# Where the TensorE fillers stand in a delta-rule recurrence: between its stages instead of behind them

## The chip, the cores and the metric

The kernel runs as one program on one core of a Trainium2 chip. The metric is the time of one execution on the device in microseconds (us); lower is better. Each engine (PE for TensorE, DVE for VectorE, ACT for ScalarE, POOL for GpSimd, SP for SyncE) takes its own instructions in the order in which they were written, and waits for other engines through semaphores.

## The reference

Three layers follow each other. The first is a recurrence over 768 tokens with a 48 x 48 state for each of 4 x 8 heads, the second a gated layer that mixes tokens, the third a gated two-layer network on neighbouring tokens.

```python
for t in range(S):                       # S = 768, B = 4, H = 8, D = 48
    y[:, :, t] = einsum('bhd,bhde->bhe', q[:, :, t], state)
    v_old = einsum('bhde,bhd->bhe', state, kt)          # kt: normalised key
    state = state + bt * einsum('bhd,bhe->bhde', kt, vt - v_old)
x = y as (B, S, 384)
h = gelu(x @ w_in)                       # 384 -> 1024, tanh form
u, v = halves of h
v_n = layer_norm(v) * g_ln
x = x + (u * (w_sg @ v_n + b_sg)) @ w_out
xk, xr = mixes of x and x one token earlier (mu_k, mu_r)
out = sigmoid(xr @ w_r) * (relu(xk @ w_k) ** 2 @ w_v)
```

## The kernel before

The recurrence is done in chunks of 64 tokens, 12 in all (`s` is 0 to 11), for two halves `o` of the 32 heads. Two chunks make a group `g` of 128 tokens, six groups in all. For a group TensorE first makes the products of its keys with each other, the Gram products (`gram`, lines 328 and 330: 64 small products for each of four quarters, each quarter in two halves `j`, copied out by ACT at line 337). VectorE then inverts a triangular matrix for each head (`solver`, background work in small pieces), and TensorE joins the result with the off-diagonal Gram blocks in two halves (`couple`, line 448, the halves of N).

For each chunk and half of the heads five stages run: `st_rq` (keys times state and keys times queries, lines 489 and 492), `st_d` (line 512), `st_n` (line 525), `st_s` (the state's update, line 540) and `st_y` (the output, line 554). Each is a burst of small products on TensorE, one 32 to 64 columns wide at a time, followed by one or two copies on ACT or DVE (`residual`, line 466, makes the operand of `st_d` from the result of `st_rq`). A float32 product of these counts twice in the trace.

The order on every engine is written by hand. Time is counted in points, 24 for a group. `run` emits one slot of three points: the stages of that slot, three calls of `tick` (which hands out background work: solver pieces, layer norm, weight rounding, and Gram products at fixed points), and at the end `fill(n)`, which emits n units of large products: `x @ w_in` of finished groups (lines 624 and 676), or, where none is ready, `keep_warm` products without use (line 715). A slot is planned for 5.315 us of TensorE time; what the stages leave of that is filled, and what is over or missing is carried on in `used[0]`. The slots of a group begin at points 0, 3, 6 ... 21, and take in turn `st_n` with `st_rq`, and `st_d` with `st_s` and `st_y`.

The weights `w_in`, `w_out` and `w_k` come in as 64-bit blocks and are rounded on the way by jobs (`narrow`): load to a tile `raw` by SP, four steps on DVE, one on POOL, a split on ACT and POOL, and for `w_out` and `w_k` a store back to DRAM by SP (`scratch`, line 197). After the recurrence come the token mixing (line 935), the projections (line 146) and the last network; the change moves nothing there.

## Time and profile before

| what | value |
|---|---|
| time, median of 3 runs | 782.36 us (777.26 to 782.89) |
| profiled execution | 785.0 us, of which the profile's span is 783.3 us |
| mean granted TensorE clock of the profiled execution | 0.961 of full speed |
| PE busy | 717.5 us of the span |
| recurrence, from the first slots to the last stage | about 54 to 349 us |

The span runs from the first to the last instruction. An execution takes some 2 us more than its span. Busy time of PE is a union of product times, of which neighbours overlap, so that a full 20 us in a window does not say that the products could not have been issued closer.

### The profile page before, as it was taken

The numbers are of one execution on the slowest core, as the hardware profiler recorded it, in microseconds if no ns is written. First come the engines' busy times: TensorE is split into PE (matmuls) and PEld (weight loads), VectorE is DVE, ScalarE is ACT, GpSimd is POOL, SyncE is SP. The second block draws the span as 40 slices with busy tenths as digits, with TensorE's granted clock in tenths as the row PEclk, the third lists the DMA queues.
The fourth block names the chain that finished last, engine by engine and source line by source line (L and its number), as shares of the span: only waits on it lengthen the run. The fifth ranks groups of instructions, "written<-read, shape, count | busy, mean of one in ns | idle before, by whom it ended". The sixth has DMA issues, their size and how long they took to land.

```text
span 783.3 us, 25096 instructions
## 1 busy us (share of the span) xinstructions
PE 717.5 (92%) x10898; PEld 658.0 (84%) x10898; DVE 504.7 (64%) x1071; ACT 373.2 (48%) x752; POOL 199.9 (26%) x246
## 2 busy tenths in 40 slices
PE   3479989899998999798889979999999999999998
PEld 3335768788887887686879969999999999999997
DVE  6997779779597895622265967269664564564441
ACT  2234566566766767753333332128463463452330
POOL 3143335344363564520216351201000000000000
PEclk9979999899799999999989989999999999999999
DMA  8312346365566647538367554228000000000000
GB/s 240 79 62 67 112 94 190 104 187 168 130 175 175 189 142 199 180 106 223 122 228 237 180 163 146 75 87 222 21 11 31 11 21 31 11 21 31 11 22 31
DMA packets 82159, 88.76 MB, mean 113 GB/s; under 512 B 24704, under 2 KB 65024, under 8 KB 82048
## 3 DMA queue, kind: packets, MB, share of 16 engines
q1 hardware_dynamic: 76816, 77.92, 33.8%
q0 software_dynamic: 4800, 9.04, 4.2%
q8 instruction: 85, 1.39, 0.8%
q10 hardware_dynamic: 432, 0.20, 0.1%
q14 instruction: 26, 0.21, 0.1%
HBM read 56.60 MB, written 25.82 MB: 105 GB/s over the span
## 4 chain that ended last, share of the span: by engine, by line
PE 75%; DMA 7%; DVE 7%; issue 3%; POOL 3%; ACT 2%; SPq 2%; POOLq 0%; DVEq 0%
PE ms L146 35%; PE ms L676 7%; PE ms L935 6%; PE ms L624 6%; PE ms L715 4%; PE ms L554 3%; PE rk L512 3%; PE rk L489 2%; PE rk L525 2%; PE sps L540 2%; PE ms L448 2%; PE ms L328 2%; DVE sg L350 1%; DMA raw<-in_w_r_dram 1%; POOL na L172 1%
## 5 line engine op out<-in xcount | busy, mean ns | idle before, releaser
L146 PE MATMUL ms<-wvh,sl 128*128 128x384 f32 x192 | 64.6, 336 | 0.0
L146 PE MATMUL ms<-wvl,sh 128*128 128x384 f32 x192 | 64.5, 336 | 0.0
L146 PE MATMUL ms<-wvh,sh 128*128 128x384 f32 x192 | 64.5, 336 | 0.0
L146 PE MATMUL ms<-xm_hi,sw0h 128*128 128x384 f32 x192 | 64.2, 335 | 0.0
L146 PE MATMUL ms<-xm_hi,sw0l 128*128 128x384 f32 x192 | 64.2, 334 | 0.0
L146 PE MATMUL ms<-xm_lo,sw0h 128*128 128x384 f32 x192 | 64.2, 334 | 0.0
L172 POOL TENSOR_TENSOR na<-na,raw 128x256 int32<-128x256 int32 (+2 forms) x43 | 38.3, 890 | 86.1 <-DVE na L170 80.4
L118 DVE TENSOR_TENSOR sl<-sg,sh 128x384 fp32r<-128x384 f32 x64 | 35.6, 557 | 30.3 <-ACT sh L115 30.2
L935 PE MATMUL ms<-sw0h,g 128*128 128x384 f32 x192 | 50.4, 336 | 2.1 <-DVE g L118 2.1
L115 ACT ACTIVATE sh<-sg 128x384 fp32r<-128x384 f32 x64 | 33.5, 524 | 36.3 <-DVE sg L1109 36.3
L935 PE MATMUL ms<-ws1h,g 128*128 128x384 f32 x192 | 49.9, 334 | 0.0
L676 PE MATMUL ms<-xh,wiu_hi 128*128 128x256 f32 x144 | 41.0, 303 | 6.9 <-ACT v L633 6.9
L1125 DVE TENSOR_TENSOR sg<-sg,ms 128x384 f32<-128x384 f32 x24 | 13.3, 554 | 46.2 <-PE ms L146 46.2
L1109 DVE TENSOR_TENSOR sg<-sg 128x384 f32<-128x384 f32 x64 | 35.3, 552 | 11.5 <-ACT sg L1108 11.4
L350 DVE TENSOR_TENSOR sg<-sg,Yt 128x512 f32<-128x512 f32 (+10 forms) x78 | 41.5, 532 | 1.6
L1108 ACT ACTIVATE sg<-ms 128x384 f32<-128x384 f32 x64 | 30.8, 481 | 24.2 <-PE ms L146 23.9
L676 PE MATMUL ms<-xl,wiu_hi 128*128 128x256 f32 x144 | 40.0, 297 | 2.4 <-issue 2.4
L115 ACT ACTIVATE gh<-w 128x384 fp32r<-128x384 f32 x32 | 16.6, 524 | 53.5 <-DVE w L1022 53.5
L676 PE MATMUL ms<-xh,wiu_lo 128*128 128x256 f32 x144 | 40.4, 299 | 0.1
L146 PE MATMUL ms<-gh,wo_hi 128*128 128x384 f32 x96 | 35.2, 366 | 5.7 <-ACT gh L115 5.7
L505 POOL TENSOR_SCALAR_AFFINE_SELECT SQ<-SQ 64x512 f32<-64x512 f32 x36 | 26.9, 746 | 48.0 <-ACT SQ L504 41.1
L676 PEld LDWEIGHTS ms<-xh,wiu_hi 128*128 128x128 f32 x144 | 27.7, 201 | 13.1 <-ACT v L633 8.2
(236 smaller groups left out, 2244.9 us busy)
## 6 DMA issues: line engine op xcount, KB each, us to landing
u_d<-ug SPq DMA_DIRECT2D x24, 256.0 KB, 4.1
u<-u_d SPq DMA_DIRECT2D x16, 384.0 KB, 5.5
vn_d<-v SPq DMA_DIRECT2D x22, 256.0 KB, 3.8
vk<-in_vk_dram SPq DMA_DIRECT2D x24, 192.0 KB, 3.9
vk<-in_vk_dram SPq DMA_DIRECT2D x12, 384.0 KB, 4.9
out_dram<-sg SPq DMA_DIRECT2D x24, 192.0 KB, 1.9
SQ<-in_q_d_dram SPq DMA_DIRECT2D x36, 96.0 KB, 3.6
xT<-yst SPq DMA_DIRECT2D x23, 144.0 KB, 3.8
```

What stands on the lines that cost most here:

```text
L115: A.activation(hi, src, AF.Copy)
L118: eng_lo.tensor_tensor(lo, src, hi.bitcast(F32), op=ALU.subtract)
L146: T.matmul(pt, lhsT=a, rhs=b, start=(i == 0), stop=(i == n - 1))
L172: G.tensor_tensor(a.bitcast(I32), a.bitcast(I32), w_lo.bitcast(I32), op=ALU.add)
L350: V.tensor_tensor(tv, vw(a_t, a_off, a_dims), vw(b_t, b_off, b_dims), op=ALU.mult)
L505: G.affine_select(out=pt, in_=pt, pattern=[[0, 8], [1, C]], compare_op=ALU.is_gt, fill=0.0, base=0, channel_multiplier=-1)
L624: T.matmul(vstat[g, b], lhsT=a[:, c], rhs=w[:, c], start=first, stop=last)
L676: T.matmul(vstat["u"][:, 2 * P * d:2 * P * d + 2 * P], lhsT=w[:, c, ds_], rhs=a[:, c].rearrange("p b t -> p (b t)"), start=first, stop=last)
L715: T.matmul(o, lhsT=warm, rhs=vw(warm, 0, [(0, 4), (1, P)]), start=True, stop=True)
L935: T.matmul(pt[:, :DM], lhsT=v[:, ds_], rhs=w, start=(c == 0 and i == 0), stop=(c == 5 and i == 2))
L1108: A.activation(r, pt[:, :DM], AF.Relu)
L1109: V.tensor_tensor(r, r, r, op=ALU.mult)
```

## The change

Nothing that is computed changes. Six edits go together:

- `run` emits the stages of a slot one after the other with a part of the filler behind each, where it emitted them together and all filler at the end. The filler of a slot is planned before it from the same costs, up to 15 units instead of 14, and split in equal parts (`gap`).
- The Gram halves and the halves of N are put in a list `batches` and emitted behind the three ticks of a slot, each followed by a part of the filler. A quarter's two halves, which followed each other, now have filler between them.
- Gram quarters come at points 13, 18, 21 and 23 of a group instead of 17, 19, 21 and 23. The plan counts them in every group, also in the last two, which have none.
- The two halves of N come 2 and 8 points after the end of the solver instead of 2 and 3.
- `raw` tiles of the rounding jobs get five buffers instead of three, in a pool of their own (`jp`), and the store of a rounded block is issued 4 points after its split instead of 2, without holding the job's place in the list of running jobs.
- The tiles `r32` and `u1` have one buffer instead of two.

```diff
-GRAM0 = 17
+GRAMS = (13, 18, 21, 23)
-PUT = 2
+PUT = 4
-GSTEP = 2
-LAGC = 2
+LAGC = (2, 8)
-NRAW = 3
+NRAW = 5
...
-            yield PUT, put
+            yield PUT, put, True
...
             for k in range(2):
-                after(LAGC + k, lambda k=k: couple(g, k))
+                after(LAGC[k], lambda k=k: join(g, k))
+
+        def join(g, k):
+            batches.append(lambda: couple(g, k))
...
-            t = ap2.tile([P, 8, D], F32, name="r32")
+            t = ap1.tile([P, 8, D], F32, name="r32")
...
-            u1 = RQs[o, "u"] = ap2.tile([P, 8, D], F32, name="u1")
+            u1 = RQs[o, "u"] = ap1.tile([P, 8, D], F32, name="u1")
...
-                        e[0] = point[0] + c[0]
+                        e[0] = point[0] + c[0] * (len(c) < 3)
...
-            if grams and (point[0] - GRAM0) % GSTEP == 0:
-                for _, f in grams.pop(0):
-                    f()
-                used[0] += 1.1
+            if grams and point[0] % 24 in GRAMS:
+                batches.extend(f for _, f in grams.pop(0))
             point[0] += 1
 
         def run(*todo):
-            bodies = [f(s, o) for f, s, o in todo]
-            used[0] += sum(COST[f.__name__[3:]] for f, _, _ in todo)
-            for _ in range(3):
-                for b in bodies:
-                    next(b, None)
+            n = point[0] % 24
+            plan = sum(k in GRAMS for k in range(n, n + 3)), n in (0, 6)
+            need = sum(COST[f.__name__[3:]] for f, _, _ in todo) + 1.1 * plan[0] + 1.4 * plan[1]
+            gap = min(max((SLOT - need + spare[0]) / 0.235, 3), 15)
+            spare[0] = min(spare[0] + SLOT - need - 0.235 * gap, 1)
+            gap /= len(todo) + 2 * plan[0] + plan[1] + (n < 3 and not todo)
+            bodies = []
+            for f, s, o in todo:
+                b = f(s, o)
+                next(b, None)
+                next(b, None)
+                bodies.append(b)
+                fill(gap)
+            for b in bodies:
+                next(b, None)
             for _ in range(3):
                 tick()
                 if early_items and point[0] >= FROM:
                     early_items.pop(0)()
-            n = min(max((SLOT - used[0]) / 0.235, 3), 14)
-            used[0] += n * 0.235 - SLOT
-            fill(n)
+            while batches:
+                batches.pop(0)()
+                fill(gap)
```

The order of instructions shows it at three places. The first is PE at the beginning of group 3 (point 0 and on), from the end of `st_rq` to the next stages; `ms<-DT,sg` is the product of N, `ms<-xh,wiu` and `ms<-wiv` are filler, `rk<-r,DT` is `st_d`, `sps` is `st_s`. Before:

```order
L489 MATMUL rk<-sw0h_120,kT_97 64x48
L492 MATMUL qk<-sw0h_120,kT_97 64x64
L489 MATMUL rk<-sw0l_121,kT_97 64x48
L492 MATMUL qk<-sw0l_121,kT_97 64x64
L448 MATMUL ms<-DT,sg_111 32x32 x64
L676 MATMUL ms<-xh,wiu_hi 128x256
L676 MATMUL ms<-xh,wiu_lo 128x256
L676 MATMUL ms<-xl,wiu_hi 128x256
```

Both halves of N, 64 products, stood in one piece; three more fillers and `st_d` followed. The same place on PE in the changed kernel:

```order
L629 MATMUL ms<-wiv_hi,xh 128x512
L629 MATMUL ms<-wiv_lo,xh 128x512
L454 MATMUL ms<-DT,sg_114 32x32 x32
L629 MATMUL ms<-wiv_hi,xl 128x512
L681 MATMUL ms<-xh,wiu_hi 128x256
L681 MATMUL ms<-xh,wiu_lo 128x256
L681 MATMUL ms<-xl,wiu_hi 128x256
L517 MATMUL rk<-r_3816,DT 32x48 x32
L681 MATMUL ms<-xh,wiu_hi 128x256
```

One half of N stands there, with two fillers ahead of it and four behind; the other half moved two slots on, and filler now also follows `st_d`.

The second place is PE at the end of `st_y` and the Gram quarter after it, in group 2 at points 21 to 23 (`ms<-sw0l` at lines 328 and 330, in the changed kernel 331 and 333, are Gram products, the lines at 676 and 629 filler). Before, its last three rows and the filler behind them:

```order
L330 MATMUL ms<-sw0l_96 32x64
L328 MATMUL ms<-sw0l_96 32x64
L330 MATMUL ms<-sw0l_96 32x64
L676 MATMUL ms<-xh,wiu_hi 128x256
L676 MATMUL ms<-xh,wiu_lo 128x256
L676 MATMUL ms<-xl,wiu_hi 128x256
```

All 64 Gram products of this slot end there in one piece; three more fillers and `st_n` followed. The same place on PE in the changed kernel, at its seam between the two quarters:

```order
L331 MATMUL ms<-sw0l_99 32x64
L333 MATMUL ms<-sw0l_99 32x64
L629 MATMUL ms<-wiv_hi,xl 128x512
L331 MATMUL ms<-sw0l_99 32x64
L333 MATMUL ms<-sw0l_99 32x64
```

A single filler stands between two pieces of 32 products each, and after the second piece `st_n` follows without filler.

The third place is SP in group 2, where it loads `raw` blocks and stores rounded ones (`wo_d<-raw`). Before:

```order
L197 DMA wo_d<-raw 256x1x192 x2
L682 DMA u_d<-ug 512x1x128 x2
L155 DMA raw<-in_w_out_dram 128x384
L155 DMA raw<-in_w_k_dram 128x512
L268 DMA vk<-in_vk_dram 64x768
```

The same stretch of SP's queue in the changed kernel:

```order
L201 DMA wo_d<-raw 256x1x192
L670 DMA vn_d<-v 128x512
L159 DMA raw<-in_w_k_dram 128x512
L670 DMA vn_d<-v 128x512
L201 DMA wo_d<-raw 256x1x192
```

Stores now stand one at a time between other transfers, and a load of a new block stands ahead of the store of an older one.

## Rows read from the trace of the kernel before

**Rows 1.** The page: busy time, the instruction queue of PE, the chain's shares.

```profile
PE 717.5 (92%) x10898; PEld 658.0 (84%) x10898; DVE 504.7 (64%) x1071; ACT 373.2 (48%) x752; POOL 199.9 (26%) x246
...
q8 instruction: 85, 1.39, 0.8%
...
PE 75%; DMA 7%; DVE 7%; issue 3%; POOL 3%; ACT 2%; SPq 2%; POOLq 0%; DVEq 0%
```

**Rows 2.** Windows, groups 1 to 5: length, engines' busy time, granted clock, DMA.

```profile
96.74:148.47 51.73, 46.77 (x1378) 39.22 (x1377) 43.34 (x99) 33.21 (x66) 22.30 (x27) 0.93 0.51 136
148.47:198.81 50.34, 45.92 (x1389) 40.03 (x1388) 39.59 (x95) 33.89 (x67) 21.92 (x29) 0.97 0.58 162
198.81:249.80 50.99, 47.86 (x1390) 42.69 (x1389) 41.35 (x94) 33.78 (x67) 22.18 (x28) 0.90 0.59 165
249.80:296.30 46.50, 46.47 (x1163) 40.75 (x1162) 39.28 (x92) 31.58 (x60) 25.85 (x29) 0.93 0.58 162
296.30:345.95 49.65, 44.98 (x1116) 37.32 (x1115) 23.40 (x44) 34.91 (x68) 22.73 (x33) 0.93 0.58 166
```

**Rows 3.** Waits of PE from 60 to 300 us: sum, times, longest.

```profile
PE ms L448 <- issue: 3.4, 2, 2.3
PE ms L328 <- issue: 3.2, 2, 2.0
PE ms L676 <- issue: 2.4, 1, 2.4
PE ms L330 <- issue: 1.4, 3, 0.7
PE ms L448 <- ACT sw0l L504: 1.3, 1, 1.3
...
PE ms L624 <- issue: 0.6, 1, 0.6
```

**Rows 4.** Timeline of PE: one such stop, inside a Gram quarter.

```profile
135.76 0.22 PE L330 MATMUL ms<-kT 64*32 64x64 f32 x1
137.97 0.24 PE L328 MATMUL ms<-kT 64*32 64x64 f32 x1 [1.98 <-issue]
```

**Rows 5.** Windows as in rows 2: a dense stretch, a clean one, one at half clock.

```profile
240.65:249.80 9.15, 6.02 (x264) 5.35 (x263) 8.46 (x11) 5.25 (x12) 2.57 (x2) 1.00 0.50 162
213.11:224.21 11.10, 11.10 (x260) 9.58 (x259) 8.86 (x18) 7.74 (x15) 6.63 (x7) 1.00 0.66 181
199.77:210.01 10.24, 10.24 (x304) 9.63 (x302) 7.72 (x34) 6.57 (x13) 3.64 (x8) 0.50 0.39 108
```

**Rows 6.** Timeline of PE: 14 fillers between two small stages, then another stage.

```profile
112.79 0.23 PE L492 MATMUL qk<-SQ,kT 64*64 64x64 f32 x2
112.95 0.50 PE L624 MATMUL ms<-wiv_hi,xh 128*128 128x512 f32 x1
113.28 0.40 PE L624 MATMUL ms<-wiv_lo,xh 128*128 128x512 f32 x1
...
116.03 0.39 PE L624 MATMUL ms<-wiv_lo,xh 128*128 128x512 f32 x1
116.34 0.88 PE L512 MATMUL rk<-r,DT 32*32 32x48 f32 x64
117.16 0.24 PE L540 MATMUL sps<-sw0h,vk 64*48 64x48 f32 x1
```

**Rows 7.** Timeline of PE: the stage of line 512 at half clock; nine keep-warm products.

```profile
105.26 1.50 PE L512 MATMUL rk<-r,DT 32*32 32x48 f32 x64
...
109.01 2.12 PE L715 MATMUL ms<-warm 128*128 128x512 bf16 x9
```

**Rows 8.** Timelines of PE and DVE: products of `st_rq` and the residual made of them.

```profile
225.94 0.23 PE L492 MATMUL qk<-SQ,kT 64*64 64x64 f32 x2
...
227.18 0.55 DVE L466 TENSOR_TENSOR r<-vk,rk 128x384 f32<-128x384 f32 x1
```

**Rows 9.** Timeline of PE behind the recurrence: the two long stops there.

```profile
371.96 0.39 PE L676 MATMUL ms<-xh,wiu_hi 128*128 128x256 f32 x1 [3.22 <-ACT v L633]
...
376.61 0.39 PE L676 MATMUL ms<-xh,wiu_hi 128*128 128x256 f32 x1 [2.25 <-ACT v L633]
```

**Rows 10.** Waits of SP from 54 to 300 us: stores of rounded blocks.

```profile
SPq L197 <- POOL raw L118: 31.1, 10, 6.5
```

More of the change, by code (lines that the diff above doesn't have):

```diff
@@ L105, in fused_kernel @@
     stg = ctx.enter_context(tc.tile_pool(name="stg", bufs=2))
+    fl = ctx.enter_context(ExitStack())
+    jp = fl.enter_context(tc.tile_pool(name="jp", bufs=2))
     xT = cp.tile([P, B, 3, S + 1], F32, name="xT")
@@ L147, in mm3, with narrow @@
                 i += 1
-    def narrow(dram, i, j, hi, lo, cw=CW, pool=stg, lag=JLAG, parts=None):
-        w = CW if pool is stg else cw
-        raw = pool.tile([P, 2 * w], U32, name="raw", bufs=NRAW if pool is stg else 2)
+    rounding = [jp]
+    def narrow(dram, i, j, hi, lo, cw=CW, lag=JLAG, parts=None):
+        pool = rounding[0]
+        w = CW if pool is jp else DM
+        raw = pool.tile([P, 2 * w], U32, name="raw", bufs=NRAW if pool is jp else 2)
         nc.sync.dma_start(out=raw[:, :2 * cw], in_=dram[i * P:(i + 1) * P, j:j + cw].bitcast(U32))
@@ L159, in narrow @@
         yield 0, lambda: A.activation(w_lo.bitcast(I32), w_lo, AF.Copy, scale=2.0 ** -29)
-        a = pool.tile([P, w], U32, name="na", bufs=NNA if pool is stg else 2)[:, :cw]
+        a = pool.tile([P, w], U32, name="na", bufs=NNA if pool is jp else 2)[:, :cw]
         af = a.bitcast(F32)
@@ L186, in resident, with scratch @@
                         for i in range(nblk) for j in range(j0, j1, CW)]
-    def scratch(dram, name, nblk, n, cw=CW, pool=stg):
+    def scratch(dram, name, nblk, n, cw=CW):
         d = dp.tile([nblk, P, 2, n], F32, name=name + "_d")
@@ L193, in job @@
             parts = []
-            yield from narrow(dram, i, j, None, None, cw, pool, parts=parts)
+            yield from narrow(dram, i, j, None, None, cw, parts=parts)
             def put():
                 nc.sync.dma_start(out=d[i, :, :, j:j + cw], in_=parts[0])
-            yield PUT, put
+            yield PUT, put, True
         return d[:, :, 0], d[:, :, 1], [lambda i=i, j=j: job(i, j) for i in range(nblk) for j in range(0, n, cw)]
@@ L218, in fused_kernel @@
     fp = tc.tile_pool(name="fp", bufs=2)
-    fl = ctx.enter_context(ExitStack())
     fp = fl.enter_context(fp)
@@ L451, in couple @@
                 A.activation(GL[r:r + 32, u0:u0 + NPR], w[r:r + 32], AF.Copy)
-            used[0] += 1.4
             joined.add(2 * g + k)
@@ L580, in store_x @@
                                     in_=yst[64 * h + e:64 * h + e + n, 6:8, :])
-        units, grams, opened, owed, splits, used = [], [], [[], None], [0], [], [0]
+        units, grams, opened, owed, splits, spare = [], [], [[], None], [0], [], [0]
         spent = [0, 0, 0]
@@ L755, in background @@
             debt[0] = min(t, 0) * (point[1] > 0)
-        running, debt = [], [0]
+        running, debt, batches = [], [0], []
         jobs = in_jobs + jobs
@@ L824, in tick @@
             point[1] = min(g, 1) + 1
-            gg, nn = divmod(point[0] - GRAM0, 24)
+            gg, nn = divmod(point[0] - GRAMS[0], 24)
             if nn == 0 and 0 <= gg and gg + 2 < NG:
@@ L978, in fused_kernel @@
     st = sx.enter_context(tc.tile_pool(name="st", bufs=1, reuse_waits="tile"))
-    wr_dh, wr_dl, j2 = scratch(w_r, "wr", 3, DM, DM, st)
-    wv_dh, wv_dl, j3 = scratch(w_v, "wv", 8, DM, DM, st)
+    rounding[0] = st
+    wr_dh, wr_dl, j2 = scratch(w_r, "wr", 3, DM, DM)
+    wv_dh, wv_dl, j3 = scratch(w_v, "wv", 8, DM, DM)
     jobs += j2 + j3
```

## The prediction

> **What bounds the kernel now.** I read the page first: PE is busy for 717.5 us of the span and holds 75% of the chain that ended last, and "issue", time in which an engine waits for nothing that the profile shows, has 3% [rows 1]. So TensorE sets the end. The change touches only the recurrence, so I cut that by groups, from one `st_n` at point 0 to the next. A group is planned at eight slots of 5.315 us, 42.5 us. Groups 1 to 3 take 51.7, 50.3 and 51.0 us; group 4, which has no Gram products, 46.5 us; group 5 takes 49.7 us [rows 2]. DVE is busy for 39 to 43 us of a group and ACT for 32 to 35 [rows 2], so neither is full, though DVE is not far from it.
>
> Two things make groups 1 to 3 long. The list of what PE waited for holds almost nothing but "issue": 3.4, 3.2, 2.4, 1.4 and 0.6 us at lines 448, 328, 676, 330 and 624, 11.0 us together, and 1.3 us put down to ACT at line 448 [rows 3]. These stops are no waits for data: one sits inside a Gram quarter, between two products of the same burst, and lasts 1.98 us [rows 4]. They come where small products are dense. The stretch with the longest stop ran 264 products in 6.02 busy us, 44 per us; a stretch without a stop ran 260 in 11.10 us, 23 per us [rows 5]. My reading is that PE uses up its instructions faster there than its queue brings them: that queue moved 85 packets [rows 1], each for 2 x 10898 / 85 = 256 of PE's instructions, weight loads counted. The second thing follows the first. The granted clock over groups 1 to 4 is 0.93, 0.97, 0.90 and 0.93 [rows 2], and in the worst stretch it is 0.50, the lower of the two levels (1.2 of 2.4 GHz), for 10.24 us, right behind a group of such stops [rows 5].
>
> **What the change removes.** (A) The stops. Filler now stands between nearly all bursts, as the first order piece shows, so the density falls towards that of the clean stretch. One dense run per group stays: at points 21 to 24 four halves of Gram follow `st_d`, `st_s` and `st_y` with a single large product between them (second order piece), and `st_n`, `st_rq` and half of N come behind. From the order that is some 420 products; at the durations of their kinds (0.82 us for the 64 of line 512 [rows 6], much the same for the others) they take a little under 11 us, 39 per us, between 44 and 23 and nearer to the dense end. I keep one stop of 0.7 us for each of three groups, 2 us. A is worth -9 us; the ends are -11 (none is left) and -4 (the dense runs stop as before).
>
> (B) The half clock behind them. Lost clock over groups 1 to 4 is 0.07 x 51.7 + 0.03 x 50.3 + 0.10 x 51.0 + 0.07 x 46.5 = 13.5 us, so 27 us at half speed. Not all work slows by two: 64 products of line 512 take 1.50 us there and 0.88 at full clock [rows 6, 7], a factor 1.7, so 41% of those 27 us, 11 us, is lost. I count group 4 in, since its low stretch starts right behind group 3's last stop. Shorter stops need not drop the clock; I keep one quarter, so B is -8.5 us, with ends -11 and -3.
>
> **What the change adds.** (C) Large products between small ones are not free at the seams. In the trace, 14 fillers stand between two stages. The first is followed after 0.33 us (112.95 to 113.28) and the last after 0.31 us (116.03 to 116.34), while those between come every 2.75 / 12 = 0.229 us [rows 6]. So each insert costs 0.10 + 0.08 = 0.18 us beyond its products. From the last small product to the next one (112.79 to 116.34) it is 3.55 us against 14 x 0.229 = 3.21, so 0.34 us, if a direct change from one small stage to the next cost nothing; it costs something, so 0.34 is the upper end, and 0.10, one seam alone, the lower. I take 0.18, which counts only what needs a large product at the seam. In the order up to the token mixing, filler stands in 49 pieces before and in 146 after. 97 x 0.18 = 17.5 us, with ends 10 and 33. There are 125 keep-warm products instead of 138; 13 at 2.12 / 9 = 0.236 us [rows 7] give back 3 us. C is +14.5 us, with ends +7 and +30. The products themselves are the same, so nothing else is added on PE. This lies on the path, because PE is not idle in the clean stretch (11.10 of 11.10 us [rows 5]).
>
> (D) The plan counts Gram quarters in groups 4 and 5 as well, 4 x 1.1 us each, so these slots get less filler. 17 fillers of 512 columns and 36 of 256 columns move behind the last stage, some 17 x 0.23 + 36 x 0.12 = 8 us. That changes no sum of PE, but it puts work where PE now waits 3.22 and 2.25 us for ACT's copies [rows 9]; I credit 4 of these 5.5 us. Against it, the slots of group 4 shrink to about 39 us of PE work while DVE alone needs 39.3 [rows 2], and in group 5 ACT needs 34.9. I charge 1 us for what gets exposed. D is -3 us, with ends -6 and +4.
>
> **What costs nothing.** The residual of `st_rq` now has about half a slot's filler ahead of `st_d`. DVE is late with it by 1.24 us at worst in what I read (last product issued at 225.94, residual begins at 227.18) and takes 0.55 us [rows 8], 1.8 us together; the order puts 2.5 us of Gram and filler there in that slot. Without that cover each such slot would wait about 1 us (second rival). `r32` and `u1` with one buffer cost nothing: the next writer comes after the next stage's own products, and PE has read the old value by then. SP stands 31.1 us in stores of rounded blocks that wait for POOL [rows 10], and loads queue behind them; later stores (third order piece) free SP, but PE never waits for a load in [rows 3], so I count 0.
>
> **The sum.** -9 - 8.5 + 14.5 - 3 = -6 us. The profiled execution took 785.0 us, which becomes 779; it lies 2.6 us above the median of the runs, and on their scale 782.4 - 6 = **776.4 us**.
>
> **The rivals.** First, the seams are cheap and the stops all go: C at its lower end (+7), A and B at -10 and -10, D -3, together -16, 766 us. For it speaks that a single filler between two bursts is first and last in one and may pay only one seam; against it, that most inserts are of three to eight. Second, on the other side: the shorter cover between `st_rq` and `st_d` is not enough. Its place is line 512 behind line 466, its price some 1 us in two of a group's four such slots over five groups, 10 us, and new half-clock stretches of about 5 us; -6 + 15 gives 791 us. It decides from the point where DVE begins the residual more than 2 us behind the last product; in the trace that is 1.24 us [rows 8], but DVE would have less slack in a shorter group. Third, the dense runs at points 21 to 24 stop as before: A -4, B -4, C and D as forecast, together +3.5, 786 us, no measurable change.
>
> The Trainium skill (Runtime: NRT & Kernel Launch, section Instruction fetch mechanics) says that an engine's instructions come in blocks of 256 while it runs and that this is hidden because issue is slower than the filling. The block size agrees with the 256 worked out above [rows 1]; that it is hidden does not fit a stop inside a burst [rows 4]. If the stops had another cause that spacing does not touch, A and B would be zero, and +14.5 - 3 gives 794 us: a fourth rival, by rows a plain "the change doesn't do what it says".
>
> **How the numbers follow.** A measurement of this kernel tells about 1% from no change, 774.5 to 790.2 us. I give the forecast (771 to 781) 0.45, the cheap seams 0.33, the third rival 0.11, short cover 0.07 and the fourth 0.04. Faster by over 1%: the 0.33 and 0.10 of the forecast's lower end, 0.43. Within 1%: 0.35 of the forecast and the third rival, 0.46. Slower: 0.11. The range leaves out the fourth rival, most of the second and the far end of the first: 763 to 788 us.
>
> **What would show it.** A: the list of PE's waits in the recurrence has under 4 us of "issue", and what is left lies at points 21 to 24. B: the granted clock of groups 1 to 3 is 0.97 or more. C: group 1 to 3 take 47 to 49 us with PE busy throughout, and a piece of few fillers shows 0.18 us beyond its products. D: the stops behind the recurrence shrink to 2 us. I am wrong if PE waits for DVE or ACT at lines 512 to 554, which is the second rival, or if "issue" stays where products are spaced, which is the fourth.

## The result and the profile after

The changed kernel takes 790.69 us (median of 7 runs, 786.3 to 791.95), the kernel before 782.36 us in the same comparison; the ratio is 1.0128, 95% interval 1.0091 to 1.0165. The change made it slower by 1.3%, and the time lies above the forecast range of 763 to 788 us.

The profiled execution took 786.3 us, 4.4 below the median, with a span of 784.6; a second profile, at 793.7 us, stands with the experiments (e16_after_again). Three single executions far longer than the others of their kernel (1708.77 us in e4_rawonly, 1524.32 in e9_stats, 888.29 in e11_alternate) are not in the ratios below, and for the last two the traces of their repeats are read, e13_stats_again and e17_alternate_again. In the changed kernel the lines lie 1 to 13 lower in the file: `couple` is at 454, the Gram products at 331 and 333, `residual` at 471, `st_rq` at 494 and 497, `st_d` at 517, `st_n` at 530, `st_s` at 545, `st_y` at 559, the filler at 629, 681 and 720, the layer norm's statistics (`ln_steps`) at 648 and 650.

Its page, busy time and the chain's shares, as in [rows 1]:

```profile
PE 718.8 (92%) x10885; PEld 643.9 (82%) x10885; DVE 515.1 (66%) x1071; ACT 371.6 (47%) x752; POOL 197.8 (25%) x246
...
PE 69%; DVE 12%; DMA 7%; POOL 4%; issue 4%; ACT 3%; SPq 1%; POOLq 0%; ACTq 0%; DVEq 0%
```

VectorE rose from 7% to 12% of the chain, and issue did not leave it. The windows of groups 1 to 5, as in [rows 2], and the stretch from the last `st_n` (345.90) to the second piece of token mixing:

```profile
94.72:148.21 53.49, 47.88 (x1376) 35.89 (x1370) 43.23 (x98) 32.70 (x65) 23.05 (x27) 0.97 0.51 132
148.21:198.78 50.57, 48.18 (x1396) 38.75 (x1389) 41.65 (x95) 33.44 (x66) 22.14 (x29) 1.00 0.59 161
198.78:247.15 48.37, 47.53 (x1391) 38.59 (x1388) 41.76 (x93) 33.52 (x66) 23.01 (x28) 1.00 0.62 173
247.15:290.29 43.14, 40.26 (x1128) 33.38 (x1122) 36.76 (x86) 28.69 (x56) 20.30 (x27) 1.00 0.56 151
290.29:345.90 55.61, 44.00 (x1077) 35.19 (x1076) 31.61 (x49) 34.97 (x69) 23.39 (x32) 0.85 0.50 141
345.90:388.44 42.54, 41.12 (x310) 38.05 (x311) 11.37 (x23) 18.00 (x32) 8.46 (x16) 1.00 0.61 169
```

Groups 1 to 3 hardly moved: 152.4 us against 153.1 [rows 2]. The clock is 0.97 to 1.00 there instead of 0.90 to 0.97, yet PE's busy time is longer (143.6 us against 140.6). Group 4 is 3.4 us shorter, group 5 is 6.0 us longer at a clock of 0.85, and the last stretch 3.1 us longer (39.45 before, from 345.95 to 385.40). From group 4's beginning to the second mixing the sum is 141.3 us against 135.6: that is where the excess of this run lies. PE's waits over the recurrence, as in [rows 3] but up to 346 us:

```profile
PE ms L454 <- DVE DT L438: 5.7, 1, 5.7
PE rk L517 <- DVE r L471: 5.3, 2, 3.5
PE ms L559 <- issue: 3.2, 2, 2.3
PE ms L720 <- ACT GL L340: 2.2, 1, 2.2
PE ms L559 <- POOL vk L461: 2.2, 2, 1.8
PE rk L517 <- issue: 1.4, 2, 1.0
```

The stops of issue fell from 11.5 to 7.6 us (in groups 1 to 3 from 11.1 to 6.1). In their place PE waits for VectorE: 5.7 us at `couple` in group 5 for the solver's transposition (line 438), 5.3 us at `st_d` for the residual.

### The profile page after: what moved, and what is told of

It is laid out like the page before. It is cut to its first block, busy times and chain, and to the rows that moved or that the text cites. A ratio compares the mean times of both kernels' runs of the same rounds, so it can differ in the third digit from the quotient of the medians.

```text
span 784.6 us, 25046 instructions
## 1 busy us (share of the span) xinstructions
PE 718.8 (92%) x10885; PEld 643.9 (82%) x10885; DVE 515.1 (66%) x1071; ACT 371.6 (47%) x752; POOL 197.8 (25%) x246
## 4 chain that ended last, share of the span: by engine, by line
PE 69%; DVE 12%; DMA 7%; POOL 4%; issue 4%; ACT 3%; SPq 1%; POOLq 0%; ACTq 0%; DVEq 0%
PE ms L147 34%; PE ms L948 7%; PE ms L629 5%; PE ms L681 5%; PE ms L720 3%; PE ms L559 3%; DVE sg L353 2%; PE rk L517 2%; PE sps L545 2%; PE rk L530 2%; PE rk L494 2%; PE ms L454 2%; DMA raw<-in_w_r_dram 1%; PE ms L331 1%; DMA raw<-in_w_v_dram 1%
## 5 line engine op out<-in xcount | busy, mean ns | idle before, releaser
L353 DVE TENSOR_TENSOR sg<-sg,Yt 128x512 f32<-128x512 f32 (+10 forms) x78 | 45.7, 586 | 1.6
L1139 DVE TENSOR_TENSOR sg<-sg,ms 128x384 f32<-128x384 f32 x24 | 13.3, 555 | 46.2 <-PE ms L147 46.2
L1123 DVE TENSOR_TENSOR sg<-sg 128x384 f32<-128x384 f32 x64 | 35.4, 553 | 11.5 <-ACT sg L1122 11.4
L168 DVE TENSOR_SCALAR na<-raw 128x256 uint32<-128x256 uint32 (+2 forms) x43 | 22.8, 531 | 25.9 <-DMA raw<-in_w_v_dram 13.7
L681 PE MATMUL ms<-xh,wiu_hi 128*128 128x256 f32 x144 | 37.8, 294 | 1.4 <-ACT v L638 1.4
L681 PE MATMUL ms<-xh,wiu_lo 128*128 128x256 f32 x144 | 38.4, 298 | 0.8 <-issue 0.8
L116 ACT ACTIVATE xm_hi<-sg 128x384 fp32r<-128x384 f32 x48 | 23.4, 517 | 31.7 <-PE ms L147 30.5
L948 PEld LDWEIGHTS ms<-sw0h,g 128*128 128x128 f32 x192 | 35.5, 192 | 3.0 <-DVE g L119 2.5
```

The source lines that it names most:

```text
L116: A.activation(hi, src, AF.Copy)
L353: V.tensor_tensor(tv, vw(a_t, a_off, a_dims), vw(b_t, b_off, b_dims), op=ALU.mult)
L681: T.matmul(vstat["u"][:, 2 * P * d:2 * P * d + 2 * P], lhsT=w[:, c, ds_], rhs=a[:, c].rearrange("p b t -> p (b t)"), start=first, stop=last)
L948: T.matmul(pt[:, :DM], lhsT=v[:, ds_], rhs=w, start=(c == 0 and i == 0), stop=(c == 5 and i == 2))
L1123: V.tensor_tensor(r, r, r, op=ALU.mult)
```

## The experiments

Every kernel was timed against the kernel before on the same chip; the ratio is to it, with its 95% interval. The rows were taken on several chips, so two rows are compared by their ratios.

| kernel | built on | median, us | ratio |
|---|---|---|---|
| changed kernel | | 790.69 | 1.0128 (1.0091 to 1.0165) |
| e16_after_again | the same | 790.2 | 1.0119 (1.0087 to 1.0152) |
| e1_plan | changed | 789.81 | 1.0106 (1.0068 to 1.0143) |
| e2_slotend | changed | 776.48 | 0.9945 (0.9912 to 0.9979) |
| e3_rawback | changed | 795.63 | 1.0171 (1.0127 to 1.0215) |
| e4_rawonly | before | 785.75 | 1.0042 (1.0005 to 1.0080) |
| e5_gramspread | e2 | 778.63 | 0.9968 (0.9935 to 1.0002) |
| e6_stagespread | changed | 787.04 | 1.0104 (1.0070 to 1.0138) |
| e7_points | e2 | 776.40 | 0.9961 (0.9928 to 0.9995) |
| e8_endplan | e2 | 779.56 | 0.9994 (0.9962 to 1.0026) |
| e9_stats | changed | 780.25 | 1.0019 (0.9987 to 1.0051) |
| e13_stats_again | the same as e9 | 782.52 | 1.0035 (1.0007 to 1.0063) |
| e14_stats_plan | e9 | 795.67 | 1.0230 (1.0184 to 1.0277) |
| e15_stats_now | e2 | 777.10 | 0.9955 (0.9920 to 0.9990) |
| e10_solver | e7 | 781.98 | 1.0044 (1.0015 to 1.0074) |
| e18_jobslate | e7 | 783.85 | 1.0047 (1.0016 to 1.0077) |
| e11_alternate | e7 | 793.32 | 1.0180 (1.0142 to 1.0219) |
| e17_alternate_again | the same as e11 | 791.01 | 1.0130 (1.0096 to 1.0163) |

**The plan, the seams, the rounding.** My first theory after the result was the plan: its phantom Gram quarters starve groups 4 and 5 of filler.

```diff
-            plan = sum(k in GRAMS for k in range(n, n + 3)), n in (0, 6)
+            plan = sum(k in GRAMS for k in range(n, n + 3)) * (point[0] < 96), n in (0, 6)
```

> The changed kernel, but the plan counts Gram quarters only in groups 0 to 3, where they exist; everything else as changed. Theory P (the slots of groups 4 and 5 are planned too short, so TensorE runs ahead of VectorE and stops for the solver's transposition and the residual): group 4 takes 45 to 47 us instead of 43.1, group 5 some 50 to 52 instead of 55.6, the stop for the transposition falls from 5.7 us to under 3, the stretch to the second mixing product shrinks by 2 to 3 us; 782 to 785 us, 6 to 8 us below the changed kernel. Rival S (the seams of the spread filler are what costs): 789 to 791 us, nothing gained. Rival V (VectorE itself sets the end of group 4 and TensorE only waits for it): the stops move into filler, only the 2 to 3 us behind the last stage come back, 787 to 789 us.

The theory fell: 789.8 us, the number of rival S. Group 4 went to 47.70 us and group 5 to 53.20, but the filler only moved; from group 4 to the second mixing it is 140.2 us against 141.3. Beside it ran the kernel with the filler back at the slot's end:

```diff
-            bodies = []
-            for f, s, o in todo:
-                b = f(s, o)
-                next(b, None)
-                next(b, None)
-                bodies.append(b)
-                fill(gap)
-            for b in bodies:
-                next(b, None)
+            bodies = [f(s, o) for f, s, o in todo]
+            for _ in range(3):
+                for b in bodies:
+                    next(b, None)
...
             while batches:
                 batches.pop(0)()
-                fill(gap)
+            fill(gap)
```

> The changed kernel with all filler of a slot at its end again and Gram quarters and halves of N in one piece behind the ticks; the points of Gram and N, the plan with its phantom quarters and the rounding jobs stay as changed. Rival S: about 100 seams of 0.18 us go, 17 us, and of the stops that come back only some 10 us are lost: 780 to 784 us. Theory P: the stops for VectorE in groups 4 and 5 stay and the issue stops of groups 1 to 3 come back to 8 us or more with granted clocks of 0.90 to 0.97: 790 to 796 us. If seams cost nothing and spacing gains what the forecast said, groups 1 to 3 here take 51 to 53 us each.

776.5 us, below what either theory gave: without the spread the rest of the change is faster than the kernel before. Its windows, from group 1 on:

```profile
96.48:146.74 50.26, 46.67 (x1372) 37.82 (x1371) 42.53 (x97) 33.33 (x66) 22.18 (x27) 0.93 0.53 142
146.74:198.29 51.55, 44.72 (x1390) 38.96 (x1390) 42.43 (x95) 33.81 (x67) 21.89 (x29) 1.00 0.56 160
198.29:244.81 46.52, 44.24 (x1390) 38.88 (x1389) 42.39 (x94) 33.52 (x67) 21.62 (x28) 1.00 0.64 182
244.81:289.22 44.41, 42.38 (x1135) 37.47 (x1134) 34.72 (x87) 30.17 (x58) 21.57 (x28) 0.92 0.53 145
289.22:338.55 49.33, 41.18 (x1102) 36.15 (x1101) 27.56 (x50) 35.70 (x70) 22.29 (x30) 0.93 0.58 169
```

PE is busy for 135.6 us in groups 1 to 3, against 143.6 in the changed kernel, for the same products of the stages and as many of filler (306). The seam itself can be read. The timeline of PE in the changed kernel, a `st_rq` ending, two fillers and a half of N:

```profile
201.41 0.22 PE L497 MATMUL qk<-sw0l,kT 64*64 64x64 f32 x1
201.56 0.50 PE L629 MATMUL ms<-wiv_hi,xh 128*128 128x512 f32 x1
201.90 0.40 PE L629 MATMUL ms<-wiv_lo,xh 128*128 128x512 f32 x1
202.22 0.25 PE L454 MATMUL ms<-DT,sg 32*32 32x32 f32 x4
```

and in e2_slotend, where the same stages follow each other directly:

```profile
160.00 0.23 PE L497 MATMUL qk<-SQ,sw0h 64*64 64x64 f32 x2
160.16 0.41 PE L454 MATMUL ms<-sw0l,GL 32*32 32x32 f32 x14
```

From 201.41 to 202.22 are 0.81 us for two fillers of 0.23, so 0.35 beyond them; a direct change of stage takes 0.16. By this pair of places an insert costs 0.19 us, the forecast's 0.18; the sums further down test it over many.

The rounding part was undone in the changed kernel, and put alone into the kernel before (with the pool `jp` and the single `r32` and `u1` that it needs):

```diff
-PUT = 4
+PUT = 2
-NRAW = 5
+NRAW = 3
...
-            yield PUT, put, True
+            yield PUT, put
```

> The changed kernel with the rounding jobs as before: three buffers of raw blocks, stores two points later, the job keeping its place until the store. Theory R (the rounding part makes VectorE and GpSimd late: a block's first step waited 2.8 us for GpSimd in group 4): 783 to 787 us, 4 us or more below the changed kernel, with the transposition's stop under 3 us. Theories P and S: within 2 us of the changed kernel, 789 to 793 us, only SyncE's waits for rounded blocks rise from 21 us towards 31.

> The kernel before with only the rounding part of the change: five buffers of raw blocks in a pool of their own, stores four points later, the place given up earlier, and the single buffers of r32 and u1 that make room. Theory R: 785 to 790 us, 3 us or more slower than before, with VectorE late at the solver. Theories P and S, and the forecast's own count of nothing: within 2 us of the kernel before, 780 to 785 us; SyncE's waits for rounded blocks fall from 31 us to about 21.

Undone in the changed kernel it doesn't help, as theory R had it: the ratio is 0.4% higher (5 us by the medians), with intervals that overlap. PE's stops at `st_d` in group 5 are 9.7 us in that profile. Alone in the kernel before it costs 0.4%, with an interval that nearly reaches zero. On the kernel without the spread it makes no difference that shows (e7_points, below).

**Which inserts.** Filler only around Gram and N, or only between the stages:

```diff
             while batches:
                 batches.pop(0)()
-            fill(gap)
+                fill(part)
```

with `part = gap / (len(batches) + 1)` and one `fill(part)` ahead of them, in e2_slotend; and in the changed kernel

```diff
-            gap /= len(todo) + 2 * plan[0] + plan[1] + (n < 3 and not todo)
+            gap /= len(todo) + (plan[0] + plan[1] > 0) + (n < 3 and not todo)
...
+            some = len(batches) > 0
             while batches:
                 batches.pop(0)()
+            if some:
                 fill(gap)
```

> The kernel e2_slotend with the filler of a slot cut only around the Gram halves and the halves of N (a part ahead of them and a part behind each), the stages still together. Inserts of filler up to the first mixing product: 86, against 51 in e2_slotend and 146 in the changed kernel. Theory S (every further insert costs some 0.19 us of TensorE time, wherever it stands): 35 x 0.19 = 6.6 us above e2_slotend's 776.5, 782 to 785 us, less 1 to 3 us if stops of issue at the Gram lines go. Rival G (the Gram and N bursts are where the stops come from, so filler there pays for itself): 773 to 777 us, with under 5 us of issue in groups 0 to 4.

> The changed kernel with filler behind each stage as changed, but the Gram halves and halves of N of a slot in one piece with one part of filler behind them. 136 inserts. Theory S: 85 x 0.19 = 16 us above e2_slotend, 790 to 794 us, as slow as the changed kernel, with TensorE busy and not waiting in groups 1 to 3. Rival W (filler between stages shortens the cover of the copies, and waits for VectorE and ScalarE are what costs): also 788 us or more, but with over 5 us of waits for VectorE or ScalarE at the stages' lines in groups 1 to 3. Theory G would put most of the cost at the stages as well, and has 12 us of issue here.

Theory G was the better one for the Gram bursts: e5_gramspread is as fast as e2_slotend within the intervals, though its 778.6 us lie between the two theories and its issue in groups 0 to 4 is 5.5 us where G had under 5. Its groups 1 to 3 are the shortest of all:

```profile
99.68:146.71 47.03, 46.67 (x1372) 36.98 (x1371) 41.30 (x93) 31.55 (x62) 19.82 (x24) 0.96 0.50 137
146.71:195.31 48.60, 46.39 (x1395) 39.07 (x1389) 42.26 (x94) 33.76 (x67) 21.87 (x29) 1.00 0.60 167
195.31:243.21 47.90, 46.50 (x1394) 39.09 (x1389) 44.55 (x96) 33.86 (x67) 22.23 (x28) 1.00 0.65 184
```

e6_stagespread, at 787 us, has nearly all of the loss. Rival W is out: in its groups 1 to 3 PE waits for ScalarE only 3.2 us, once, and not for VectorE. The 12 us of issue that theory G gave it are not there either: with the Gram bursts in one piece it has 4.4 us in groups 1 to 3, so filler between the stages thins the stops too, at the price of more inserts.

What is left of the change without spread and rounding (e2_slotend with the rounding diff above), and e2_slotend with the right plan (the plan's diff above):

> The kernel e2_slotend with the rounding jobs as before: what is left of the change is the points of Gram and N, the plan made ahead with its phantom quarters, and the single buffers. If the points carry the gain over the kernel before: 775 to 778 us, as e2_slotend. If the rounding part carries it in this order (its undoing cost the changed kernel 5 us): 780 to 784 us, as the kernel before.

> The kernel e2_slotend with the plan that counts Gram quarters only where they exist. Theory V (VectorE's solver sets the end of group 4, so filler there only replaces the stop at the transposition, 6.3 us in e2_slotend): within 2 us of e2_slotend, 774.5 to 778.5 us, the stop at the transposition shorter by 2 us or more and the stretch from the last stage to the first mixing product shorter by as much. Theory P: 770 to 773 us.

776.4 us: the points of Gram and N, with the plan made ahead, carry the gain. The right plan doesn't help: 779.6 us is above what either theory gave and 0.5% above e2_slotend by the ratios, whose intervals barely overlap.

Then fewer inserts than before, the filler of two slots put together (built on e7_points):

```diff
-            fill(gap)
+            saved[0] += gap
+            if n % 6 == 0:
+                fill(saved[0])
+                saved[0] = 0
```

> The kernel e7_points with the filler of two slots put together behind the slot of st_n and st_rq, none behind st_d, st_s and st_y: 26 inserts instead of 51. Theory S carried on below: 25 x 0.19 = 4.8 us less, 771 to 774 us, if stops stay. Theory F of the forecast (dense small products make TensorE stop for its instructions and halve the clock): issue stops grow from 12 us by half or more, more stretches at half clock, 778 to 785 us.

> The kernel e11_alternate once more, since its profiled execution was disturbed: it took 793 us where seams alone gave 771 to 774. Theory F (dense small products make TensorE stop for its instructions and halve the clock): issue stops in groups 0 to 4 at 18 us or more, against 12 in e7_points and e2_slotend, and 40 us or more at half clock. Rival W (without filler behind st_y the next stages wait for copies): 10 us or more of waits for ScalarE or VectorE in groups 0 to 4.

791 us in the second trial. Groups 1 to 3, windows and the largest of PE's waits of issue:

```profile
95.37:151.51 56.14, 49.52 (x1384) 41.16 (x1378) 42.52 (x99) 33.41 (x65) 21.34 (x26) 0.88 0.46 126
151.51:202.81 51.30, 45.42 (x1393) 40.46 (x1388) 41.51 (x95) 33.74 (x66) 22.17 (x29) 0.97 0.57 160
202.81:256.94 54.13, 47.19 (x1394) 41.65 (x1389) 43.23 (x93) 33.88 (x66) 22.58 (x28) 0.94 0.56 155
```

```profile
PE ms L454 <- issue: 4.8, 3, 1.9
PE rk L494 <- issue: 3.3, 4, 1.7
...
PE ms L333 <- issue: 2.0, 2, 1.3
```

Both trials lie above what either theory gave. In groups 0 to 4 the stops of issue grew, 16.5 us against 11.6 in e7_points, short of the 18 that theory F asked for, and waits for ScalarE are 3.8 us, so rival W is out. The half clock there is 30.7 us against 8.4, where F had 40; that it comes with the density isn't shown, since e18_jobslate, with e7's order of filler, has 28.5.

**Groups 1 to 3 in terms.** With inserts counted in each trace, 0.19 us for each, the stops, and 41% of the time at half clock (the forecast's factor), each against the kernel before:

| kernel | inserts | issue, other stops, half clock (us) | terms, sum | measured |
|---|---|---|---|---|
| before | 24 | 11.1, 1.3, 20.5 | | (153.1 us) |
| changed | 78 | 6.1, 2.7, 3.4 | +10.3 -5.0 +1.4 -7.0 = -0.3 | -0.6 |
| e16_after_again | 78 | 6.3, 2.4, 6.8 | +10.3 -4.7 +1.1 -5.6 = +1.1 | +2.0 |
| e2_slotend | 24 | 10.1, 2.3, 6.8 | 0 -1.0 +1.0 -5.6 = -5.6 | -4.7 |
| e5_gramspread | 48 | 3.3, 0.6, 3.4 | +4.6 -7.8 -0.7 -7.0 = -10.9 | -9.5 |
| e6_stagespread | 72 | 4.4, 3.5, 3.4 | +9.1 -6.7 +2.2 -7.0 = -2.4 | -3.2 |
| e17_alternate_again | 12 | 13.3, 5.9, 23.9 | -2.3 +2.3 +4.6 +1.4 = +6.0 | +8.5 |

The four terms account for each kernel within 2.5 us, and for ten more profiles of these experiments within 1.1. The stops go with the order: 5.1 to 7.1 us of issue in the six profiles with the spread of the changed kernel, 7.5 to 10.1 with the new points and the filler at the slot's end. The half clock doesn't: with the filler at the slot's end e7_points has 3.4 us, e2_slotend 6.8, e15_stats_now 10.2, e10_solver 17.1 and e18_jobslate 23.9. The windows of groups 1 to 3 in e18_jobslate, where TensorE has the order of e2_slotend:

```profile
94.27:146.93 52.66, 48.13 (x1371) 39.22 (x1370) 41.67 (x97) 33.46 (x66) 21.68 (x27) 0.90 0.51 138
146.93:196.50 49.57, 45.80 (x1389) 39.72 (x1388) 40.70 (x95) 33.84 (x67) 21.81 (x29) 0.97 0.57 158
196.50:249.50 53.00, 48.40 (x1389) 42.86 (x1388) 40.56 (x91) 33.27 (x66) 22.68 (x28) 0.90 0.62 167
```

**VectorE behind the gelu.** In groups 4 and 5 VectorE's list of waits has one entry that the kernel before hardly has (1.7 us there):

```profile
DVE st L648 <- ACT v L638: 13.8, 4, 4.7
```

All four lie in group 5, at 305.44, 310.80, 335.97 and 340.41. The first two on VectorE's timeline, and the solver's transposition ahead of them:

```profile
297.45 1.95 DVE L438 STREAM_TRANSPOSE DT<-sg 128x1024 f32<-128x1024 f32 x1
...
305.44 0.69 DVE L648 BATCH_NORM_STATS2 st<-v 128x6 f32<-128x512 f32 x1 [4.35 <-ACT v L638]
...
310.80 0.69 DVE L648 BATCH_NORM_STATS2 st<-v 128x6 f32<-128x512 f32 x1 [4.66 <-ACT v L638]
```

With filler emitted ahead of the ticks, a block of v that ends in it gets its statistics from a tick of the same slot, where it used to be the next slot's. VectorE stands at that instruction until PE has done the filler and ScalarE the gelu, with the solver and the residual queued behind. Three points later:

```diff
-            streams.append([point[0] + 1, ln_steps(g, b, v), "ln"])
+            streams.append([point[0] + 4, ln_steps(g, b, v), "ln"])
```

> The changed kernel with the statistics of the layer norm handed to VectorE three points later, nothing else. With filler ahead of the ticks of its slot, a finished block of v now gets its statistics into VectorE's queue in the same slot, and VectorE stands there until ScalarE has done the gelu: 13.8 us in groups 4 and 5, against 1.7 us in the kernel before. Rival B (this blocks VectorE, and the residual is late in group 5 because of it): the stops at the residual, 3.5 us, and for the vk block, 1.8 us, go below 1 us together, group 5 takes 51 to 53 us instead of 55.6, 784 to 787 us. Theory S (seams) and theory V (VectorE's work up to the transposition): VectorE's idle time moves elsewhere, 789 to 792 us.

> The kernel e9_stats once more, since its profiled execution was disturbed and shows no stage as it is. If the statistics' place in VectorE's queue was the cause: 777 to 784 us again; VectorE's wait for gelu at the statistics in groups 4 and 5 under 4 us instead of 13.8, the stops of TensorE at the residual and the vk block in group 5 under 1.5 us together instead of 5.3, group 5 at 50 to 53 us instead of 55.6.

> The changed kernel as it is, once more: its only profile is its fastest run, 786.3 us, 4.4 us below its median, so part of the excess has not been seen in a trace. Theory B (VectorE blocked by the gelu and late in group 5): a profile at the median shows groups 4 and 5 with the stretch to the second mixing product at 143 to 147 us instead of 141.3, by longer stops for VectorE at the transposition or the residual. Theory S alone: the excess lies in groups 1 to 3, 2 us or more longer than in the first profile.

This one number takes 0.9 to 1.1% away by the ratios, 7 to 9 us (the medians are 780.25 and 782.52 us), about half of the 1.8% that the spread costs over e2_slotend. The second profile of the changed kernel (e16_after_again), groups 4, 5 and the stretch behind:

```profile
252.44:296.56 44.12, 41.21 (x1128) 34.14 (x1122) 35.78 (x85) 28.55 (x56) 20.28 (x27) 0.96 0.52 142
296.56:351.95 55.39, 43.86 (x1077) 34.99 (x1076) 31.83 (x49) 34.91 (x69) 23.34 (x32) 0.85 0.49 141
351.95:395.22 43.27, 41.12 (x310) 38.06 (x311) 11.38 (x23) 18.00 (x32) 8.47 (x16) 1.00 0.60 166
```

and with the statistics later (e13_stats_again):

```profile
249.12:295.34 46.22, 43.15 (x1129) 35.81 (x1122) 36.01 (x87) 28.26 (x57) 19.33 (x25) 0.93 0.58 162
295.34:343.88 48.54, 41.06 (x1077) 33.08 (x1076) 27.56 (x48) 34.36 (x68) 25.30 (x33) 0.93 0.55 161
343.88:385.30 41.42, 41.12 (x311) 38.06 (x311) 12.02 (x23) 19.40 (x34) 8.65 (x18) 1.00 0.60 174
```

Group 5 is 6.9 us shorter and the three stretches 6.6 us (136.2 against 142.8). The wait for the gelu is gone from VectorE's list. My number for the stops was wrong, though: 4.3 us at the transposition and 2.9 at the residual stay in group 5; what went is 4 us of stops (11.5 to 7.5) and 10 us at half clock (17.1 to 6.8). The second profile of the changed kernel also shows group 5 as in the first (55.4 and 55.6 us); what made its run longer lies mostly ahead of group 4, in groups 0 to 3. Groups 1 to 3 are 2.7 us longer, the sign of theory S, and the stretch from group 4 on, 142.8 us, stays just short of the 143 to 147 of theory B.

So the statistics' place costs this much. That the wait for the gelu is what costs isn't shown. All four waits come behind the transposition, so the longest stop of PE isn't theirs:

```profile
299.54 0.69 PE L454 MATMUL ms<-DT,GL 32*32 32x32 f32 x18 [5.74 <-DVE DT L438]
```

The faster e2_slotend, where VectorE waits for the gelu only once in these groups, for 3.1 us at 337.44, has that stop too, but a shorter one at the residual. PE's waits in its group 5:

```profile
PE ms L454 <- DVE DT L438: 6.3, 1, 6.3
PE rk L517 <- DVE r L471: 1.3, 1, 1.3
```

The changed kernel's stop at the residual in group 5 (3.5 us, to 331.31) follows a wait of VectorE for ScalarE at line 119, 4.3 us up to 326.55, for a piece of the mixing's weights. And the later place also delays what follows the statistics on POOL and ScalarE (lines 658 to 665); the two were not tried apart.

The converse, the blocking put into a kernel that hasn't the spread, and the plan put right once VectorE is free:

```diff
-            streams.append([point[0] + 1, ln_steps(g, b, v), "ln"])
+            body = ln_steps(g, b, v)
+            next(body)
+            streams.append([point[0] + 1, body, "ln"])
```

> The kernel e2_slotend, all filler at the slot's end, with the statistics put into VectorE's queue right at the gelu's place, about one point earlier: the suspected cost added to a kernel that hasn't the spread. Rival B: VectorE waits for the gelu for 8 us or more in groups 4 and 5, the residual and the next transposition come late, 782 to 788 us against 776.5. If only filler between the stages makes the blocking harmful: 775 to 779 us.

> The kernel e9_stats with the plan that counts Gram quarters only where they exist. Theory P in its second form (the short slots of groups 4 and 5 cost only once VectorE is no longer blocked): 774 to 778 us. Theory V (VectorE's work up to the transposition of group 5 sets that point whatever TensorE does): within 2.5 us of e9_stats, 778 to 783 us, as the same edit did nothing on the changed kernel (789.8 against 790.7).

In e15_stats_now VectorE waits for the gelu only 4.7 us in groups 4 and 5, of the 8 expected. The time stays at 777.1, within the range of the second reading (only filler between the stages makes the blocking harmful), but the dose was too small to tell. In e14_stats_plan both theories missed: the two edits together are slower than either, 795.7 us. PE stops once for 6.1 us at `st_d` in group 5:

```profile
312.10 1.50 PE L517 MATMUL rk<-r,DT 32*32 32x48 f32 x64 [6.14 <-DVE mv L650]
```

VectorE's timeline ahead of that:

```profile
300.15 0.81 DVE L168 TENSOR_SCALAR na<-raw 128x256 uint32<-128x256 uint32 x1 [4.77 <-POOL raw L119]
...
309.10 0.68 DVE L648 BATCH_NORM_STATS2 st<-v 128x6 f32<-128x512 f32 x1
309.70 0.54 DVE L471 TENSOR_TENSOR r<-vk,rk 128x384 f32<-128x384 f32 x1
310.15 1.90 DVE L438 STREAM_TRANSPOSE DT<-sg 128x1024 f32<-128x1024 f32 x1
```

`st_d` reads the residual, done at 310.24, and the transposition DT, done at 312.05, so it is the transposition that came last. VectorE is busy without a gap from 300.15 on and comes to it late, behind a rounding block that waited 4.8 us for POOL and two statistics, which e13_stats_again, without the fuller plan, doesn't have there. My reading, which no run shows by itself, is that it matters what stands on VectorE's queue just ahead of the residual and the transposition.

**Is VectorE the bound at group 5?** Twice the solver's share, or no new rounding blocks in group 4, both on e7_points:

```diff
-SHARE = ((1, 4, 1), (1, 4, 1), (2, 8, 2))
+SHARE = ((1, 4, 1), (1, 4, 1), (2, 16, 2))
```

```diff
-            if point[0] < LASTP and jobs and len(running) < RUN[1 + late] and n % (2 if late else EVERY) == 0:
+            if point[0] < LASTP and not 90 <= point[0] < 114 and jobs and len(running) < RUN[1 + late] and n % (2 if late else EVERY) == 0:
```

> The kernel e7_points with twice the share of VectorE's background time for the solver in groups 1 to 4 (16 against 2 and 2, instead of 8). Theory V: the transposition of group 5 comes 2 us or more earlier after that of group 4 than the 48.0 us of e7_points, its stop of 4.4 us shrinks to under 2, 773 to 776 us. If rounding and layer norm, now later, are what TensorE waits for behind it: 776 to 780 us, with new stops for ScalarE or GpSimd in group 5. If the share has no hold on the time, since the solver's pieces already come first: within 1 us of e7_points.

> The kernel e7_points with no new rounding job begun from points 90 to 113, so that VectorE does five blocks less, some 7 us, between the transpositions of groups 4 and 5; they follow later. Theory V (VectorE's work up to the transposition sets the beginning of group 5): the two transpositions stand 44 us or less apart instead of 48.0, TensorE's stop there, 4.4 us, shrinks below 1, 772 to 775 us; faster than every kernel so far if the blocks find room behind. If TensorE or the blocks' later place takes it back: 775 to 779 us.

Neither gained: both are slower than e7_points, by 0.8 and 0.9% by the ratios. With the larger share the two transpositions stand 48.9 us apart (48.0 in e7_points) and PE's stop is 4.0 us. Without the rounding blocks the stop for the transposition in group 5 is gone, but one of 2.9 us stands in group 4 instead, and the transpositions are still 49.3 us apart, since group 4 is 6 us longer:

```profile
249.50:297.33 47.83, 43.00 (x1197) 37.53 (x1197) 37.82 (x79) 29.43 (x53) 15.57 (x21) 0.95 0.45 128
297.33:342.67 45.34, 40.46 (x1038) 35.20 (x1037) 23.82 (x46) 34.61 (x69) 23.18 (x31) 0.94 0.53 151
```

So theory V, that VectorE's amount of work alone sets the beginning of group 5, is not borne out; both kernels also take longer behind the second mixing, where 4 and 3 more rounding blocks now stand (the spans are 787.1 us each, e7_points has 772.2; the medians are 5.6 and 7.5 us apart from its).

## Why the prediction was wrong, point by point

**The step that failed is D,** and A was sized too large. D charged 1 us for what the short slots of groups 4 and 5 expose on VectorE and ScalarE. In the profile PE's stops in these two groups grew from 4.6 to 14.3 us: 5.7 for the transposition, 5.3 for the residual, 1.8 for POOL and 1.5 of issue. Group 5 runs at a clock of 0.85 (17 us at half speed), and from group 4 on the kernel loses 5.7 us (7.2 in the second profile) where D, the seams there (29 inserts, 5.2 us) and B's share of group 4 (2.1 us) came to about zero. The credit was right, the stops behind the recurrence shrank from 6.1 to 1.4 us, and so was the shape of group 4, 43.1 us. But I took the wrong thing to be the danger. The phantom quarters cost nothing that shows (e1_plan). What the forecast doesn't name is an order: filler ahead of the ticks moves the layer norm's statistics a slot earlier on VectorE's queue. Moving them back takes 7 to 9 us of time away, about half of the 14 us by which the forecast missed. I read the order of PE and SP around the change, not that of VectorE. Much of the rest lies in groups 1 to 3, where A, B and C were to come to -5.7 us and came to -0.6 and +2.0 in the two profiles.

**C, the seams,** was right in its price (0.19 against 0.18 us) and count (54 more inserts in groups 1 to 3). It took 10 us in groups 1 to 3, all that the other terms gave there.

**A, the stops,** came to -5.0 us in groups 1 to 3, from 11.1 to 6.1, where -9 was forecast and the lower end was -4; I had kept 2 us. The sign that I had named, under 4 us of issue in the recurrence, was missed with 7.6, and the 47 to 49 us for each group with 53.5 and 50.6. Of what is left 3.2 us stand at line 559 in the last slot of a group, at points 21 to 24 as said, 1.4 at line 517 elsewhere.

**B, the half clock,** was right in groups 1 to 3 of both profiles: 20.5 us at half speed became 3.4 and 6.8, worth -7.0 and -5.6. Which edit brought it stays open. e2_slotend, with the filler at the slot's end, has 6.8, but three more kernels with the filler there have 10.2 to 23.9, and the seven profiles with filler between the stages 3.4 to 10.2; with one profile for most kernels, part of it may be luck. In the changed kernel group 5 gives part of it back.

**What was put at nothing.** The rounding part is nearly that: +0.4% alone, and no difference clear of the noise with the spread or without it. The residual's cover held in groups 1 to 3, where PE did not wait for VectorE at all; in groups 4 and 5 it waited twice, 5.3 us in all, because VectorE itself was late.

**The rivals.** The second came closest in time (791) and in place (line 512, now 517), but not in its reason: no waits in two slots of every group, but two in all, with VectorE late. The first is out, since seams cost their full price. The third was half right, the stops at points 21 to 24. The fourth is out: spacing does change the stops, 13.3 us of issue at 12 inserts in groups 1 to 3, 10.1 at 24, 3.3 at 48 around the Gram bursts, 4.4 at 72 and 6.1 at 78. The Trainium skill (Runtime: NRT & Kernel Launch, section Instruction fetch mechanics) holds that fetching is hidden; these traces show stops that move with the density of small products, though not that fetching is their cause, which was not measured by itself.

**Still open:** by which path the earlier statistics lengthen group 5. The stops that went with them (4 us) and the half clock (10.3 us, worth 4.2) add up to the 6.9 us of group 5 with some left over. But the waits for the gelu lie behind the transposition, e15_stats_now could not produce the blocking, and e14_stats_plan shows that another order of the same queue is worse still.

**A version that beats both:** e2_slotend, 776.5 us, 0.55% (0.21 to 0.88) faster than the kernel before, with e7_points and e15_stats_now alike within their intervals.

## What to carry to other kernels

Filler that is cut into more pieces costs 0.19 us for each on TensorE in this kernel; it pays only by the stops that it takes away. In groups 1 to 3, 24 more inserts around the Gram bursts cost 4.6 us and took 6.8 us of issue away (e5_gramspread against e2_slotend); 48 more, nearly all between the stages, cost 9.1 and took 5.7 (e6_stagespread). Neither made the whole kernel faster. When filler moves, follow what its end triggers on the other engines: here a statistics instruction went a slot earlier into VectorE's queue, and its place was worth 7 to 9 us. Before crediting spacing for a better clock, take the spacing away alone, and look at more than one profile: with one order of TensorE the half clock of groups 1 to 3 ranged from 3.4 us (e7_points) to 23.9 (e18_jobslate).

## What the runs showed of the hardware

The same instruction on VectorE took very different times in one trace, as line 168 on 128 x 256 elements with 0.27 and 1.62 us in group 4 of the changed kernel. The long one, from 272.72 on, stands beside an instruction of POOL (line 119, 272.50 to 274.19). The solver's products at line 353 took 586 ns on the mean against 532 in the kernel before; what stretches them was not tried, and in the faster e7_points they are longer still (602 ns). The stops of issue are not bound to the Gram bursts: one of 2.29 us stands in the middle of a `st_y` (between its first 16 products and its last 16, up to 143.40 us).
